# A block of the second layer without the seven-product scheme, and the weights' sums moved into it

## The chip, the cores and the metric

One Trainium2 chip, one core. The metric is the device time of one execution in microseconds (us). The kernel before took 956.48 us, the median of three runs (952.09 to 957.19).

## The reference

A decayed linear attention over 4 batches, 8 heads, 768 positions of 48 channels is followed by two feed-forward layers on 3072 tokens of width 384, with 2048 hidden channels. All inputs and outputs are float32.

```
state = alpha[t, :, None] * state + k[t] (x) v[t];   y[t] = q[t] . state
h = x @ w_in;  g = P3(h) / (1 + |b0||h| + |b1| h^2);  x = g @ w_out      # first layer
h = x @ w_in;  g = h * cos(h);                         out = g @ w_out     # second layer
```

The second layer's weights arrive in a 64-bit format and are converted on the chip.

## The kernel before, in words

**Tiling.** Tokens are cut into six blocks of 512 (`TB`), hidden channels into 16 tiles of 128. One step n of `layers(n)` stands for one hidden tile of one block: steps 0 to 95 are the first layer, steps 96 to 191 the second. Block b of the second layer has the steps 96 + 16b to 111 + 16b, so that block 1 is 112 to 127 and block 2 is 128 to 143. `f` is the place of the step in its block.

**One step.** Each float32 operand is kept as two fp32r words, high and low, and a product of two operands is three passes. `gemm1(n)` writes the hidden tile h(n) into a PSUM bank: nine matmuls of 512 columns in the plain form. `cosine(n)` works on earlier tiles: in the plain form the angle of tile n-1 (ScalarE L78, VectorE L79), and for tile n-2 the sine (ScalarE L744), the product with h (VectorE L746, the last reader of h), the high word (ScalarE L688) and the low word (GpSimd L693). `second(n)` runs `gemm2` for the tile that is `lag` steps back: 4 in the plain form, 5 in the other. A `gemm2` is nine matmuls of 512 columns.

**The seven-product form.** Where `by_seven(n)` holds, two steps (an even one and the odd one after it) share their sub-products: instead of 18 matmuls of 512 columns, `seven` issues six of 512 and 21 of 256. The even step issues six of 256 into bank `r0` ahead of its gemm2 (`seven(n, 0)`), ScalarE moves them out (L604), and after the gemm2 six more go into the same bank (`seven(n, 1)`), which ScalarE moves out as well (L610). The odd step issues the rest into two banks `h_bank(n-1)` and `h_bank(n)`. GpSimd (L605, L616, L618) and VectorE (L627) add what was moved out. The tiles' angle and sine are one step later than in the plain form.

**What the form needs.** Sums of the block's x (`x_sums0` at f = 10, `x_sums1` at f = 14 of the block before; for block 1 on GpSimd at f = 10 of block 0 and at f = 0 of block 1), and sums of the weights, which serve blocks 1 to 5 (`weights_sums(j)` for the pair of tiles 2j, 2j+1). Before, block 0 is plain, block 1 is plain up to f = 3 and in the seven-product form from f = 4, and a whole pair of weights' sums is made in each odd step of block 1: two VectorE additions of 128x256 (L515), four VectorE additions of 128x128 (L519 to L522), then twice a ScalarE copy (L524) and a GpSimd subtraction (L525).

**Weights.** The last weights of the second layer (`w_out`, tiles up to f = 15) are still converted in block 0 and the first steps of block 1: `tick(3)` at the end of each step issues ScalarE L67 and L68, VectorE L72 and L73, the next step ScalarE L187 and GpSimd L196. `words_bank` gives the conversion a free PSUM bank in the steps 100 to 109; later ones work in place in SBUF.

**Order.** The program is issued in the order of the code on every engine, and an engine runs its instructions in that order. A tile that is allocated under a tag whose single buffer an older tile holds can be written first when all readers of the older tile are through, those that come later in the code on other engines too. PSUM banks have one buffer each.

Of the kernel before, what the change touches and what calls it, by code (L numbers as in the profile page):

```python
# [9 lines left out]
F32 = mybir.dt.float32  # L10
F32R = mybir.dt.float32r
# [3 lines left out]
ALU = mybir.AluOpType  # L15
# [3 lines left out]
NC, C = 6, 128  # L19
HP = 4  # L20
NF = DFF // 128
# [18 lines left out]
def attn_then_two_moe(ctx, tc, kqT, aT, vP, w1i, w1o, ma, mb, w2i, w2o, out):  # L40
    nc = tc.nc
# [40 lines left out]
    const = main.enter_context(tc.tile_pool(name="const", bufs=1))  # L82
# [8 lines left out]
    def temp(tag, dtype=F32, shape=(128, TB)):  # L91

        bufs = {"z": 3, "ah": 2, "g": 4, "hi": 3, "lo": 3}[tag]
        return el.tile(list(shape), dtype, tag=tag, name=tag, bufs=bufs)

    def bank(tag, shape=(128, TB), dtype=F32):

        return ps.tile(list(shape), dtype, tag=tag, name=tag)
# [14 lines left out]
    ws = [[wp.tile([128, 2, DM], F32R, name=f"w{s}_{i}") for i in range(NF)] for s in range(2)]  # L113
# [13 lines left out]
    LEAD = NU - 4  # L127
    slot = [0]
# [23 lines left out]
    def words_bank(w):  # L152

        if slot[0] < LEAD:
            return words_t
        if N1 + 3 < slot[0] - LEAD < N1 + NF - 2:
            return bank(f"r{w[2] % 2}", (128, TB), I32)[:, :DM]
        return None

# [297 lines left out]
    N1 = NC * NF  # L457
    N1 = NC * NF
# [5 lines left out]
    def where(n):  # L464
        m, r = divmod(n, N1)
        if n < 2 * H1:
            return 0, *divmod(n, H1)
        if n < 2 * NF:
            blk, f = divmod(n - 2 * H1, NF - H1)
            return 0, blk, H1 + f  # L470
        return m, *divmod(r, NF)
# [8 lines left out]
    HT = TB // 2  # L480
    PASSES = ((0, 0), (0, 1), (1, 0))
    s_in = {}
    x_t = {}
    held = {}

    def by_seven(n):

        m, blk, f = where(n)
        return m == 1 and 0 < blk and (blk > 1 or f >= 4) and (blk < NC - 1 or f < NF - 2)

    def lag(n):

        return 5 if n < N1 or by_seven(n) else 4

    def h_bank(n):
        if n < N1 + NF:
            return bank(f"b{n % 3}")
        return bank((("b1", "b2"), ("r1", "b0"))[n % 2][n // 2 % 2])

    def weights_sums(j):  # L500

        if j == 2:
            held["s1"] = [const.tile([128, 128], F32R, tag=f"s{i}", name=f"s1_{i}") for i in range(2)]
        if j < 6:
            flat = held["kq"][:, 2 * DM * j:2 * DM * (j + 1)].rearrange("p (a b c) -> p a b c", a=2, b=3)
            s = [flat[:, i] for i in range(2)]
        else:
            s = [
                const.tile([128, 3, 128], F32R, tag=f"v{2 * (j - 6) + i}", name=f"s_in{j}{i}") for i in range(2)
            ]  # L510
        first = held["s1"] if j == NF // 2 - 1 else [ws[0][2 * j + 1][:, i, 0:128] for i in range(2)]
        a = temp("z", shape=(128, 4, 128))
        for i in range(2):
            w = ws[0][2 * j + i].bitcast(F32)
            nc.vector.tensor_tensor(  # L515
                out=a[:, 2 * i:2 * i + 2].rearrange("p a b -> p (a b)"), in0=w[:, 0, 0:256], in1=w[:, 1, 0:256], op=ALU.add
            )
        t = temp("g", shape=(128, 4, 128))
        nc.vector.tensor_tensor(out=t[:, 0], in0=a[:, 2], in1=a[:, 3], op=ALU.add)  # L519
        nc.vector.tensor_tensor(out=t[:, 1], in0=t[:, 0], in1=a[:, 0], op=ALU.subtract)  # L520
        nc.vector.tensor_tensor(out=t[:, 2], in0=a[:, 0], in1=a[:, 2], op=ALU.subtract)
        nc.vector.tensor_tensor(out=t[:, 3], in0=a[:, 1], in1=t[:, 1], op=ALU.subtract)  # L522
        for hi, lo, of in ((first[0], first[1], t[:, 0]), (s[0], s[1], t[:, 1:])):
            nc.scalar.activation(out=hi, in_=of, func=AF.Copy)  # L524
            nc.gpsimd.tensor_tensor(out=lo, in0=of, in1=hi.bitcast(F32), op=ALU.subtract)  # L525
        s_in[j] = [[first[i]] + [s[i][:, k] for k in range(3)] for i in range(2)]

    def x_sums0(blk):

        raw = xt[1, blk][:, 1].bitcast(F32)  # L530
        t = [in_p.tile([128, TB], F32, tag="p", name="t") for _ in range(2)]
        eng = nc.gpsimd if blk == 1 else nc.vector
        eng.tensor_tensor(
            out=t[0].rearrange("p (a b) -> p a b", a=2), in0=raw[:, 0:2, HT:],
            in1=raw[:, 0].rearrange("p (a b) -> p a b", a=2), op=ALU.subtract,
        )
        eng.tensor_tensor(out=t[1][:, :HT], in0=raw[:, 1, HT:], in1=t[0][:, :HT], op=ALU.subtract)
        eng.tensor_tensor(out=t[1][:, HT:], in0=raw[:, 1, :HT], in1=t[1][:, :HT], op=ALU.subtract)
        held["t"] = t

    def x_sums1(blk):

        t = held.pop("t")
        if blk == 1:
            held["kq"] = const.tile([128, 5 * 2 * HP * C], F32R, tag="kq", name="s_in")
        tag, words = (("st", 4 * DM), ("a", 3 * HP * (C + 1)))[blk % 2]
        to = const.tile([128, words], F32R, tag=tag, name=f"x_t{blk}")[:, :6 * HT].rearrange(
            "p (a b c) -> p a b c", a=2, b=3
        )
        if 1 < blk < NC - 1:  # L550
            first = [xt[1, blk][:, i, 0, HT:] for i in range(2)]
        else:
            first = [held["kq"][:, 12 * DM + HT * i:12 * DM + HT * (i + 1)] for i in range(2)]
        x_t[blk] = [[first[i]] + [to[:, i, k] for k in range(3)] for i in range(2)]
        for hi, lo, of in (
            (first[0], first[1], t[0][:, :HT]), (to[:, 0, 0], to[:, 1, 0], t[0][:, HT:]),
            (to[:, 0, 1:], to[:, 1, 1:], t[1].rearrange("p (a b) -> p a b", a=2)),
        ):
            nc.scalar.activation(out=hi, in_=of, func=AF.Copy)
            nc.vector.tensor_tensor(out=lo, in0=of, in1=hi.bitcast(F32), op=ALU.subtract)  # L560
# [242 lines left out]
    def all_ok1():  # L803
        cnt = bank("r1", (1, 2 * NU))
        nc.tensor.matmul(cnt, ones, ok.rearrange("p a b -> p (a b)"), start=True, stop=True)
        tot = const.tile([1, 1], F32, name="tot")
        nc.vector.tensor_reduce(tot, cnt, mybir.AxisListType.X, ALU.add)
        nc.vector.tensor_scalar(bad, tot, 128.0 * 2 * NU - 0.5, None, ALU.is_lt)


    def layers(n):
        slot[0] = n + LEAD
        if n == N1 + 4:
            gemm2(N1 - 1)
            done[0] += 1
        if n < 2 * N1:
            gemm1(n)
        if n == NF:
            all_ok0()
        if n == NF + 2:  # L820
            all_ok1()
        m, r = divmod(n, N1)
        blk, f = divmod(r, NF)
        nxt = (m, blk + 1) if blk + 1 < NC else (m + 1, 0)
        at, load = f - 11, f == 8
        if n < NF:
            nxt, at, load = (0, 1), n - 5, n == 3
        elif n < 2 * NF:
            at, load = f - 12, f == 10
        split = 0 <= at < NK and n < 2 * N1 and nxt[0] < 2  # L830
        rational(n)
        cosine(n)
        w_hi()
        if split:
            x_hi(*nxt, at)
        second(n)
        if n < 2 * N1 and by_seven(n) and n % 2 == 0:
            seven(n, 1)
            seven_out1(n)
        if m == 1 and blk == 1 and f % 2:  # L840
            weights_sums((f + 3) // 2 % (NF // 2))
        if m == 1 and nxt[0] == 1 and f == 10:
            x_sums0(nxt[1])
        if n < 2 * N1 and nxt[0] < 2 and load:
            for kk in range(NK):
                x_load(*nxt, kk)
        if split:
            x_lo(*nxt, at)
        if m == 1 and nxt == (1, 2) and f == 0:
            x_sums1(1)  # L850
        if m == 1 and nxt[0] == 1 and nxt[1] > 1 and f == 14:
            x_sums1(nxt[1])
        i = n - (N1 - NF)
        if n < 2 * NF:
            if n > 1:
                w_fetch(2 * NF)
                tick(1 if n > 2 else 0, 1)
        elif n < N1 - NF:
            w_fetch(3 * NF + NO)
            if not split:  # L860
                tick(1, 1)
        elif n < N1:
            w_fetch(4 * NF)
            if i > 3:
                tick(1, 1)
        else:
            w_fetch(4 * NF)
            tick(3 if n > N1 + 3 else 1, 1)
        if 0 <= i < NF:
            w_load(i)  # L870
        if 0 <= i - 6 < NO:
            w_load(NF + i - 6)
        w_lo([nc.gpsimd])
# [248 lines left out]
```

## Time and profile before

| what | value |
|---|---|
| median of three runs | 956.48 us |
| the profiled execution's own time | 956.72 us |
| its span, first to last instruction | 955.0 us |
| VectorE, ScalarE, GpSimd busy | 742.3, 696.4, 730.6 us |
| TensorE waits for ScalarE L604, total of three | 7.8 us |
| TensorE waits for GpSimd L196, one | 3.8 us |
| mean granted clock of TensorE | 0.980 |

The span is what the trace covers; 1.72 us of the execution lie around it. A granted clock of 1.00 is TensorE's upper level, 2.4 GHz, and 0.50 the lower one, 1.2 GHz; a stretch between them has some of both. Matmuls are pipelined, so the start of one is 0.23 us behind the start of the one before although each is drawn 0.40 us long.

### The profile page before, as it was taken

How to read it: one execution, taken by the hardware profiler on the slowest of the kernel's cores; microseconds unless marked ns; L12 is line 12 of the kernel's file. 1: busy time of each engine (PE TensorE's matmuls, PEld its weight loads, DVE VectorE, ACT ScalarE, POOL GpSimd, SP SyncE). 2: the span in 40 equal slices, each digit the busy share in tenths (PEclk: the TensorE clock that was granted, in tenths of full speed). 3: DMA queues.
4: the chain of work that ended last, by engine and by line, in shares of the span. 5: the costliest groups of instructions: out<-in, count | busy, mean ns of one | idle time of the engine just before them, and what ended most of it. 6: DMA issues, size and time to landing. Idle time of an engine off the chain costs nothing. (4 is left out here: it accounts for less than half of the span.)

```text
span 955.0 us, 15338 instructions
## 1 busy us (share of the span) xinstructions
PE 914.6 (96%) x5309; PEld 755.8 (79%) x5309; DVE 742.3 (78%) x1219; ACT 696.4 (73%) x1276; POOL 730.6 (77%) x690
## 2 busy tenths in 40 slices
PE   8797899999999999999999999888899999999997
PEld 7676777878888888888888888677788888888885
DVE  7988979999999989989989656769647658567442
ACT  5888987878779788878888777555566666656663
POOL 5888998989889989879878656576666666666662
PEclk7999999999999999999999999899999999999999
DMA  8999941111113122131265242010010010100001
GB/s 285 312 318 308 295 117 34 34 34 34 66 67 100 34 100 66 67 116 51 63 218 157 78 141 89 18 66 1 1 67 1 1 67 1 66 1 1 34 1 37
DMA packets 47029, 84.68 MB, mean 89 GB/s; under 512 B 5504, under 2 KB 22144, under 8 KB 46944
## 3 DMA queue, kind: packets, MB, share of 16 engines
q1 hardware_dynamic: 46944, 83.62, 27.0%
q8 instruction: 44, 0.72, 0.3%
q14 instruction: 41, 0.34, 0.1%
HBM read 63.15 MB, written 20.45 MB: 88 GB/s over the span
## 5 line engine op out<-in xcount | busy, mean ns | idle before, releaser
L658 PE MATMUL acc<-hi,w 128*128 128x512 f32 x1152 | 393.0, 396 | 3.8 <-POOL w L196 3.8
L693 POOL TENSOR_TENSOR lo<-g,hi 128x512 fp32r<-128x512 f32 x192 | 257.5, 1341 | 102.6 <-ACT hi L688 96.2
L642 PE MATMUL b<-x,w 128*128 128x512 f32 x1053 | 266.5, 398 | 0.6 <-DVE g L711 0.5
L658 PEld LDWEIGHTS acc<-hi,w 128*128 128x128 f32 x1152 | 217.3, 189 | 52.6 <-POOL w L196 4.2
L642 PEld LDWEIGHTS b<-x,w 128*128 128x128 f32 x1053 | 198.2, 189 | 50.0 <-DVE g L711 2.1
L658 PE MATMUL acc<-lo,w 128*128 128x512 f32 x576 | 228.1, 396 | 0.0
L688 ACT ACTIVATE hi<-g 128x512 fp32r<-128x512 f32 x192 | 121.3, 632 | 98.9 <-DVE g L724 51.5
L719 POOL TENSOR_TENSOR z<-z,ah 128x512 f32<-128x512 f32 x96 | 127.2, 1324 | 8.0
L658 PEld LDWEIGHTS acc<-lo,w 128*128 128x128 f32 x576 | 108.6, 188 | 23.1
L746 DVE TENSOR_TENSOR g<-ah,b 128x512 f32<-128x512 f32 x76 | 51.9, 682 | 70.2 <-ACT ah L744 67.8
L79 DVE SCALAR_TENSOR_TENSOR ah<-z,b 128x512 f32<-128x512 int32 x76 | 52.0, 684 | 42.9 <-ACT z L78 42.6
L720 DVE TENSOR_TENSOR g<-g,b 128x512 f32<-128x512 f32 x96 | 65.4, 682 | 25.0 <-ACT g L717 24.3
L718 POOL TENSOR_SCALAR z<-ah,cq 128x512 f32<-128x512 f32 x96 | 74.9, 780 | 1.1 <-ACT ah L716 1.1
L717 ACT ACTIVATE g<-b,cq 128x512 f32<-128x512 f32 x96 | 74.6, 777 | 0.0
L724 DVE SCALAR_TENSOR_TENSOR g<-g,cq,r 128x512 f32<-128x512 f32 x96 | 71.0, 740 | 0.1
L711 DVE SCALAR_TENSOR_TENSOR g<-g,cq,b 128x512 f32<-128x512 f32 x96 | 70.8, 738 | 0.0
L744 ACT ACTIVATE ah<-ah,half_pi 128x512 f32<-128x512 f32 x96 | 68.7, 716 | 0.0
L728 ACT ACTIVATE r<-z,lnb 128x512 f32<-128x512 f32 x96 | 66.7, 695 | 1.8 <-POOL z L719 1.6
L713 DVE SCALAR_TENSOR_TENSOR r<-z,r 128x512 f32<-128x512 f32 x96 | 65.8, 686 | 0.0
L708 DVE SCALAR_TENSOR_TENSOR z<-z,r 128x512 f32<-128x512 f32 x96 | 65.1, 678 | 0.0
L716 ACT ACTIVATE ah<-b 128x512 f32<-128x512 f32 x96 | 56.5, 588 | 7.5 <-PE b L642 7.1
L568 PE MATMUL b<-x,w 128*128 128x256 f32 (+1 forms) x276 | 61.8, 355 | 0.0
(161 smaller groups left out, 1614.3 us busy)
## 6 DMA issues: line engine op xcount, KB each, us to landing
kq<-kqT SPq DMA_DIRECT2D x24, 512.0 KB, 5.5
raw<-w2i SPq DMA_DIRECT2D x16, 384.0 KB, 3.0
w<-wd SPq DMA_DIRECT2D x16, 384.0 KB, 3.1
raw<-w2o SPq DMA_DIRECT2D x16, 384.0 KB, 3.1
v<-vP SPq DMA_DIRECT2D x24, 192.0 KB, 5.4
x<-x0d SPq DMA_DIRECT2D x18, 256.0 KB, 3.5
x1d<-o SPq DMA_DIRECT2D x18, 256.0 KB, 2.1
x<-x1d SPq DMA_DIRECT2D x18, 256.0 KB, 3.7
```

The source lines that it names most:

```text
L642: nc.tensor.matmul(h, ws[0][f][:, w, ks], x[:, xx, kk, :], start=i == 0, stop=i == 8)
L658: nc.tensor.matmul(acc[k], ws[1][f][:, w, ks], d[g], start=first and i == 0, stop=last and i == 2)
L688: nc.scalar.activation(out=t["hi"], in_=t["g"], func=AF.Copy)
L693: eng.tensor_tensor(out=t["lo"], in0=t["g"], in1=t["hi"].bitcast(F32), op=ALU.subtract)
L711: nc.vector.scalar_tensor_tensor(g, g, cq[:, 3:4], two["h"], ALU.add, ALU.mult)
L713: nc.vector.scalar_tensor_tensor(r, z, -2.0 / LN_S, r, ALU.add, ALU.mult)
L717: nc.scalar.activation(out=g, in_=h, func=AF.Identity, scale=cq[:, 5:6], bias=cq[:, 4:5])
L718: nc.gpsimd.tensor_scalar(zz, ah, cq[:, 1:2], cq[:, 0:1], ALU.mult, ALU.add)
L719: nc.gpsimd.tensor_tensor(out=zz, in0=zz, in1=ah, op=ALU.mult)
L724: nc.vector.scalar_tensor_tensor(g, g, cq[:, 2:3], r, ALU.add, ALU.mult)
L728: nc.scalar.activation(out=r, in_=two["z"], func=AF.Ln, scale=LN_S, bias=lnb)
L744: nc.scalar.activation(out=t["r"], in_=t["r"], func=AF.Sin, bias=half_pi)
```

## The change

Block 1 is plain in all its steps (`by_seven` asks for a block above 1, and `h_bank` rotates over three banks up to step 127). The sums of x for block 1 are no longer made. The weights' sums begin at step 115 (f = 3 of block 1) and take two steps a pair: the odd step makes the two large additions on VectorE and the four small ones on GpSimd, the even step after it the copies on ScalarE and the subtractions on GpSimd. The last of the eight pairs ends at step 130. `words_bank` gives a PSUM bank up to step 126.

```diff
-        if N1 + 3 < slot[0] - LEAD < N1 + NF - 2:
+        if N1 + 3 < slot[0] - LEAD < N1 + 2 * NF - 1:
             return bank(f"r{w[2] % 2}", (128, TB), I32)[:, :DM]
...
-        return m == 1 and 0 < blk and (blk > 1 or f >= 4) and (blk < NC - 1 or f < NF - 2)
+        return m == 1 and 1 < blk and (blk < NC - 1 or f < NF - 2)
...
     def h_bank(n):
-        if n < N1 + NF:
+        if n < N1 + 2 * NF:
             return bank(f"b{n % 3}")
         return bank((("b1", "b2"), ("r1", "b0"))[n % 2][n // 2 % 2])
 
-    def weights_sums(j):
-
-        if j == 2:
+    def weights_sums0(j):
+
+        a = temp("z", shape=(128, 4, 128))
+        for i in range(2):
+            w = ws[0][2 * j + i].bitcast(F32)
+            nc.vector.tensor_tensor(
+                out=a[:, 2 * i:2 * i + 2].rearrange("p a b -> p (a b)"), in0=w[:, 0, 0:256], in1=w[:, 1, 0:256], op=ALU.add
+            )
+        held["sums"] = t = temp("g", shape=(128, 4, 128))
+        nc.gpsimd.tensor_tensor(out=t[:, 0], in0=a[:, 2], in1=a[:, 3], op=ALU.add)
+        nc.gpsimd.tensor_tensor(out=t[:, 1], in0=t[:, 0], in1=a[:, 0], op=ALU.subtract)
+        nc.gpsimd.tensor_tensor(out=t[:, 2], in0=a[:, 0], in1=a[:, 2], op=ALU.subtract)
+        nc.gpsimd.tensor_tensor(out=t[:, 3], in0=a[:, 1], in1=t[:, 1], op=ALU.subtract)
+
+    def weights_sums1(j):
+
+        if j == 0:
+            held["kq"] = const.tile([128, 5 * 2 * HP * C], F32R, tag="kq", name="s_in")
             held["s1"] = [const.tile([128, 128], F32R, tag=f"s{i}", name=f"s1_{i}") for i in range(2)]
...
-        t = temp("g", shape=(128, 4, 128))
-        nc.vector.tensor_tensor(out=t[:, 0], in0=a[:, 2], in1=a[:, 3], op=ALU.add)
...
+        t = held.pop("sums")
         for hi, lo, of in ((first[0], first[1], t[:, 0]), (s[0], s[1], t[:, 1:])):
             nc.scalar.activation(out=hi, in_=of, func=AF.Copy)
             nc.gpsimd.tensor_tensor(out=lo, in0=of, in1=hi.bitcast(F32), op=ALU.subtract)
...
-        if m == 1 and blk == 1 and f % 2:
-            weights_sums((f + 3) // 2 % (NF // 2))
-        if m == 1 and nxt[0] == 1 and f == 10:
+        at_sums = n - N1 - NF - 3
+        if 0 <= at_sums < NF:
+            (weights_sums0, weights_sums1)[at_sums % 2](at_sums // 2)
+        if m == 1 and nxt[0] == 1 and nxt[1] > 1 and f == 10:
             x_sums0(nxt[1])
...
-        if m == 1 and nxt == (1, 2) and f == 0:
-            x_sums1(1)
```

## Rows read from the trace of the kernel before

**Rows 1.** The page's part 1: busy time, share of the span, instructions.
```profile
PE 914.6 (96%) x5309; PEld 755.8 (79%) x5309; DVE 742.3 (78%) x1219; ACT 696.4 (73%) x1276; POOL 730.6 (77%) x690
```
**Rows 2.** Waits of TensorE: us in total, times, longest us.
```profile
PE r L568 <- ACT q L604: 7.8, 3, 2.7
PE acc L658 <- POOL w L196: 3.8, 1, 3.8
```
**Rows 3.** Windows: stretch, its us, busy us (x instructions) by engine, TensorE clock.
```profile
core 0: us, PE busy (x) PEld busy (x) DVE busy (x) ACT busy (x) POOL busy (x), PEclk, DMA share, GB/s
...
596.96:601.15 4.19, 4.19 (x19) 3.38 (x18) 3.25 (x5) 2.51 (x7) 1.76 (x2) 1.00 0.26 77
...
605.36:614.99 9.63, 5.88 (x20) 4.36 (x19) 6.74 (x12) 5.95 (x12) 5.71 (x6) 0.77 0.00 0
614.99:620.23 5.24, 5.24 (x19) 4.19 (x18) 4.18 (x9) 1.99 (x5) 3.53 (x4) 0.78 0.00 0
```
**Rows 4.** Windows over pairs of seven-product steps: 120, 124, 128 and 130.
```profile
636.35:646.77 10.42, 7.79 (x38) 6.69 (x36) 8.18 (x18) 5.57 (x11) 6.96 (x8) 0.84 0.00 0
...
654.84:667.14 12.30, 9.88 (x47) 8.24 (x46) 11.53 (x20) 7.14 (x15) 8.80 (x8) 0.86 0.00 0
...
675.20:687.77 12.57, 9.85 (x47) 8.24 (x45) 9.07 (x17) 6.58 (x12) 8.17 (x8) 0.86 0.01 1
687.77:695.83 8.06, 8.06 (x47) 7.00 (x45) 3.72 (x6) 4.63 (x8) 5.33 (x5) 1.00 0.00 0
```
**Rows 5.** GpSimd's timeline: start, us, line, tile, [idle before <- releaser].
```profile
573.97 1.31 POOL L533 TENSOR_TENSOR t<-x 128x512 f32<-128x512 f32 x1
...
600.27 1.29 POOL L693 TENSOR_TENSOR lo<-g,hi 128x512 fp32r<-128x512 f32 x1 [2.43 <-ACT hi L688]
601.53 1.21 POOL L196 TENSOR_TENSOR w<-st,w 128x384 fp32r<-128x384 f32 x1
...
610.47 1.31 POOL L196 TENSOR_TENSOR w<-st,w 128x384 fp32r<-128x384 f32 x1
```
**Rows 6.** VectorE's timeline: a conversion in a bank, one in place, x's sums.
```profile
588.29 0.55 DVE L72 SCALAR_TENSOR_TENSOR r<-st,r 128x384 int32<-128x384 int32 x1
...
592.11 1.44 DVE L72 SCALAR_TENSOR_TENSOR st<-st,raw 128x384 int32<-128x384 int32 x1 [1.49 <-ACT raw L68]
...
601.77 1.85 DVE L560 TENSOR_TENSOR x_t<-t,x_t 128x256 fp32r<-128x256 f32 x2
```
**Rows 7.** ScalarE's timeline at steps 116 and 123.
```profile
621.54 0.59 ACT L604 ACTIVATE q<-r 128x512 f32<-128x512 f32 x1
...
657.82 0.31 ACT L524 ACTIVATE s<-g 128x128 fp32r<-128x128 f32 x1 [2.04 <-DVE g L519]
```
**Rows 8.** All engines' timeline where the odd step 117 begins.
```profile
623.74 1.20 PE L568 MATMUL b<-x,w 128*128 128x512 f32 x6
624.00 0.60 ACT L610 ACTIVATE z<-r 128x512 f32<-128x512 f32 x1 [0.86 <-PE r L568]
624.49 0.71 ACT L744 ACTIVATE ah<-ah,half_pi 128x512 f32<-128x512 f32 x1
...
625.31 0.69 DVE L746 TENSOR_TENSOR g<-ah,b 128x512 f32<-128x512 f32 x1 [1.97 <-ACT ah L744]
```
**Rows 9.** TensorE's timeline in the attention: two of its idle stretches.
```profile
31.44 0.67 PE L336 MATMUL u<-v,g 128*64 128x48 f32 x16 [1.01 <-DVE s L346]
...
43.18 0.67 PE L336 MATMUL u<-v,g 128*64 128x48 f32 x16 [2.95 <-DVE pc L261]
```
**Rows 10.** Windows behind those idle stretches; the clock is before DMA share.
```profile
31.00:34.00 3.00, 2.56 (x48) 2.37 (x48) 2.55 (x10) 2.97 (x8) 3.00 (x4) 1.00 0.72 158
...
44.00:50.00 6.00, 6.00 (x50) 5.11 (x51) 3.92 (x10) 5.08 (x11) 4.32 (x6) 0.50 0.95 305
```
**Rows 11.** The weights' sums by line: duration ns min/median/max.
```profile
L515 DVE TENSOR_TENSOR z<-w x16: 410/581/1518, 605.8 to 677.7; 128x256 f32<-128x256 f32 x16
...
L525 POOL TENSOR_TENSOR s_in<-g,s_in x8: 996/1004/1110, 609.5 to 679.8; 128x384 fp32r<-128x384 f32 x8
L525 POOL TENSOR_TENSOR w<-g,w x7: 453/623/627, 608.3 to 678.9; 128x128 fp32r<-128x128 f32 x7
```

More of the change, by code (lines that the diff above doesn't have):

```diff
@@ L511, in weights_sums @@
         first = held["s1"] if j == NF // 2 - 1 else [ws[0][2 * j + 1][:, i, 0:128] for i in range(2)]
[L512 to L517, printed above, removed]
-        t = temp("g", shape=(128, 4, 128))
-        nc.vector.tensor_tensor(out=t[:, 0], in0=a[:, 2], in1=a[:, 3], op=ALU.add)
-        nc.vector.tensor_tensor(out=t[:, 1], in0=t[:, 0], in1=a[:, 0], op=ALU.subtract)
-        nc.vector.tensor_tensor(out=t[:, 2], in0=a[:, 0], in1=a[:, 2], op=ALU.subtract)
-        nc.vector.tensor_tensor(out=t[:, 3], in0=a[:, 1], in1=t[:, 1], op=ALU.subtract)
+        t = held.pop("sums")
         for hi, lo, of in ((first[0], first[1], t[:, 0]), (s[0], s[1], t[:, 1:])):
@@ L531, in x_sums0 @@
         t = [in_p.tile([128, TB], F32, tag="p", name="t") for _ in range(2)]
-        eng = nc.gpsimd if blk == 1 else nc.vector
-        eng.tensor_tensor(
+        nc.vector.tensor_tensor(
             out=t[0].rearrange("p (a b) -> p a b", a=2), in0=raw[:, 0:2, HT:],
@@ L536, in x_sums0 @@
         )
-        eng.tensor_tensor(out=t[1][:, :HT], in0=raw[:, 1, HT:], in1=t[0][:, :HT], op=ALU.subtract)
-        eng.tensor_tensor(out=t[1][:, HT:], in0=raw[:, 1, :HT], in1=t[1][:, :HT], op=ALU.subtract)
+        nc.vector.tensor_tensor(out=t[1][:, :HT], in0=raw[:, 1, HT:], in1=t[0][:, :HT], op=ALU.subtract)
+        nc.vector.tensor_tensor(out=t[1][:, HT:], in0=raw[:, 1, :HT], in1=t[1][:, :HT], op=ALU.subtract)
         held["t"] = t
@@ L543, in x_sums1 @@
         t = held.pop("t")
-        if blk == 1:
-            held["kq"] = const.tile([128, 5 * 2 * HP * C], F32R, tag="kq", name="s_in")
         tag, words = (("st", 4 * DM), ("a", 3 * HP * (C + 1)))[blk % 2]
@@ L549, in x_sums1 @@
         )
-        if 1 < blk < NC - 1:
+        if blk < NC - 1:
             first = [xt[1, blk][:, i, 0, HT:] for i in range(2)]
```

## The prediction

> **What bounds the kernel now.** I began with the page's engines: TensorE's matmuls cover 96% of the span, the next engine 78% [rows 1]. So the time is TensorE's work plus its stalls. The waits of TensorE, read next, name four stalls in the layers that exceed 2 us: three before line L568 that end with ScalarE's L604, 7.8 us together, and one before L658 that ends with GpSimd's L196, 3.8 us [rows 2]. The timeline put all four around the steps that change, so I laid windows over them.
>
> A plain step takes 4.20 us: step 112 starts at 596.96 and step 114 at 605.36, 8.40 for two. Steps 114 and 115 then take 9.63 and 5.24, 6.47 more than two plain steps [rows 3]. An undisturbed pair of seven-product steps takes 8.06, as at 687.77; the pairs from steps 120, 124 and 128 take 10.42, 12.30 and 12.57 [rows 4]. Each loss is larger than its wait, because the granted clock is 0.84 to 0.86 in these windows and 0.77 and 0.78 in those of steps 114 and 115: the matmuls behind an idle stretch ran partly at 1.2 GHz. The pair of step 128 loses 4.51 us with a wait of 2.7, so the clock took 1.8; at steps 114 and 115 it took about 2.7 (6.47 less 3.8).
>
> Steps 116 to 127 lie between 620.23 [rows 3] and 675.20 [rows 4]: 54.97 us.
>
> **The change part by part.**
>
> *Plain steps for 116 to 127.* Twelve plain steps are 50.40 us instead of 54.97: 4.57 less. Of that, the form itself goes the other way: six pairs at 8.40 instead of 8.06 cost 2.04. What is won is the stalls. The stall of step 120 is made by the change of lag from 4 to 5: in that step no gemm2 is due, so nothing lies between the two halves that share bank r0, and TensorE waits for L604. Those of steps 124 and 128 come from ScalarE: L524 of the odd step before stands ahead of L604 and waits, 2.04 us at 657.82, for VectorE's small additions [rows 7]. A plain step has no L604 and needs a tile's words only four steps later, so a late ScalarE there reaches no matmul at once.
>
> *The stall of step 114.* The low word of the w_out tile for gemm2 at f = 14 is written by GpSimd at 610.47 to 611.78. The one before began at 601.53, so 8.94 us passed where TensorE's step took 4.20 [rows 5]. In between, VectorE made x's sums for block 1 (1.85 for two of the three) and a weights' sum, and GpSimd waited for both chains; two conversions had run in place, 1.44 against 0.55 in a bank [rows 6]. After the change all of that is gone from steps 106 to 114: the three GpSimd instructions (the first 1.31 [rows 5]), three copies and three subtractions of x's sums, the weights' sums of step 113, and the in-place conversions. With an interval of 4.20 the word would be done at 601.53 + 4.20 + 1.31 = 607.0, and TensorE asked for it at 611.8 - 3.8 = 608.0 [rows 2]; the earlier intervals shrink too, so I expect no wait: 6.47 less. Bounds: 6.47 if it goes, 0 if the chain is as late for another reason.
>
> *The weights' sums, later and in two steps.* Their VectorE and ScalarE instructions are the same but for the four small additions, which go to GpSimd. No row shows such an addition there; the nearest, L525 of the same 128x128, takes 0.45 to 0.63 with a median of 0.62, and 128x384 takes 1.00 [rows 11]. I take 0.62. GpSimd's work for two plain steps is then 2 x 1.29 for L693 [rows 5], 0.62 + 1.00 for L525 and 4 x 0.62: 6.68 of 8.40, so it stays beside TensorE, at nothing. If that cover is gone, the adds cost up to what they take (E below); a gain from a lighter VectorE is left out, since no plain step waits for it. VectorE has for two plain steps four instructions of 0.69 (L746 and L79; the row of L746 [rows 8]) and two L515 of 0.41 to 1.52 [rows 11], 5.8 at most of 8.40. Steps 122 to 127 carry x's sums and splits for block 2 besides, as before. No moved piece issues a DMA; the queue of SP is not passed.
>
> *A new wait at step 129.* `h_bank(127)` is now `b1` (127 mod 3 is 1), and `h_bank(128)` is `b1` too. Bank b1 is written at the start of step 129, before the last reader of tile 127's h, which is VectorE's L746 of the same step. TensorE must wait for it, with gemm2(125) behind it in its queue. The chain is read from step 117: TensorE goes on at 623.74, ScalarE starts L610 at 624.00, L744 at 624.49, and L746 runs from 625.31 to 626.00 [rows 8]. There nobody waited for that; here it is 626.00 - 623.74 = 2.26, with 0.08 to be seen. After L610 now stand the two L524 of the pair that ends in step 128, one of them 0.31 [rows 7], the other of 384 columns and so between that and the 0.60 of L610. That is 0.91 at most; since L744 begins 0.11 before L610 ends, I count 0.7 (an estimate). The idle time is 3.04. The clock falls behind it, as behind the stall of 2.95 in the attention, where it was 0.50 for the next 6 us [rows 9, 10]; 1.8 to 2.7 by the cases above, I take 1.9, and 4.9 in all. Bounds: 0, if L746 came sooner than I read, and 5.7.
>
> *The lag moves to step 132.* There no gemm2 is due now. The pair loses 2.10 of work (half of 4.20), which the pair of step 120 lost before, and TensorE waits for L604. The block's outputs stand ahead of it on ScalarE, as at step 116, where L604 ran from 621.54 to 622.13 [rows 7] while the pair had begun at 620.23 [rows 3]. Its first six matmuls are as much as three of the 18 in a step of 4.20, 0.70: with 0.07 for the signal 622.20 - 620.93 = 1.27 idle. An idle stretch of 1.01 left the clock at 1.00 [rows 9, 10], so I add nothing for it; 1.8 is the other bound.
>
> *The sum.* Steps 114 and 115: -6.47. Steps 116 to 127: -4.57. Steps 128 to 131: 12.57 + 8.06 = 20.63 [rows 4] becomes 16.12 + 4.9 = 21.02: +0.39. Steps 132 and 133: 8.06 becomes 8.06 - 2.10 + 1.27 = 7.23: -0.83. Together -11.5. The profiled execution took 956.72 (955.0 and 1.72 around it), 0.24 above the median of 956.48; 956.72 - 11.5 = 945.2.
>
> **The rivals.**
>
> *B, no wait at step 129.* For it: L744 and L746 need nothing of step 129 but their place behind L610. Against: that place is fixed by the code, and L610 ends after TensorE is ready. Time: 945.2 - 4.9 = 940.3.
>
> *C, one or two stalls are left in steps 122 to 128.* VectorE makes x's sums for block 2 there, and L604 of step 128 follows. For it: the stalls of 124 and 128 sat here. Against: ScalarE no longer waits for the small additions in the same step. Each costs what they did, 4.3: 949.5 or 953.8.
>
> *D, the conversion is still late at step 114.* For it: it had under 1 us to spare with an interval of 4.20. Against: what lengthened the intervals is gone. Time: 945.2 + 6.47 = 951.7, half of this on either side of the bound below.
>
> *E, GpSimd's additions hold VectorE: slower.* In the rows L515, with both operands in SBUF, takes 0.41 to 1.52 for one shape [rows 11]. If every addition on GpSimd holds VectorE for its 0.62, eight pairs of four are 19.8 us; if all of it came to TensorE the time would be 965.0. It is slower than before by over 0.5% only if 16.1 of the 19.8 come through. Against: VectorE has 8.40 - 5.8 = 2.6 us to spare in a pair, and 2.5 are asked; only around steps 122 to 127 is there too little.
>
> The Trainium skill (SBUF — State Buffer, section "Who interferes with whom") speaks for E: a VectorE instruction with two SBUF inputs and a GpSimd instruction that reads SBUF exclude each other for a whole instruction, while one with at most one SBUF input is free of this. By the first half the additions on GpSimd would cost E's price at worst; by the second, L746 and L79, which read h from PSUM, go on, and the sum stays at 945.2. The trace bears out that an instruction with two SBUF inputs varies (0.41 to 1.52) and L746 shows 0.69.
>
> **How the numbers follow.** A 0.62, B 0.08, C 0.18 (0.14 one stall, 0.04 two), D 0.07, E 0.05. The likeliest gives 945.2. The range of 939.5 to 951.5 takes in B, A with its bounds and one stall of C, and leaves out two stalls, over half of D, and E, about 0.13. A measurement of this kernel can tell about 0.5% from no change, 4.8 us: faster means under 951.7. A, B, one stall of C and half of D are faster: 0.87; two stalls and the other half of D the same: 0.08; E slower: 0.05.
>
> **What would show it.** In the changed kernel's waits of TensorE, L658 behind L196 is gone, and steps 112 to 128 follow each other by 4.20 with the clock at 1.00. At step 129 a wait of about 3 us for VectorE's L746 stands before L568, with a clock below 1.00 behind it. At step 132 a wait of about 1.3 us for L604. L525 and the additions fit into GpSimd's steps with idle time left. The prediction is wrong if TensorE waits in steps 114 to 128, if step 129 shows no wait, or if the stretch from step 134 on changes its 8.06 a pair.

## The result, and the profile after

The changed kernel took 942.39 us, the median of four runs (940.65 to 943.57), against 955.63 for the four runs of the kernel before that stood beside them (952.09 to 957.19): a ratio of 0.9865 with a 95% interval of 0.9832 to 0.9898. The forecast was 945.2. Four more executions, beside a second set of the kernel before, are under E1.

The profiled execution took 940.65, its span is 938.8, the mean granted clock 0.993. The changed kernel's line numbers have moved: L568 of before is L570, L604 is L606, L610 is L612, L658 is L660, L693 is L695, L744 is L746, L746 is L748; L515 is L505, the four small additions are L509 to L512, L524 and L525 are L529 and L530.

TensorE's waits in the layers answer to [rows 2]; two of over 1 us are left, and both are new:

```profile
PE b L570 <- DVE g L748: 2.8, 1, 2.8
...
PE r L570 <- ACT q L606: 1.1, 1, 1.1
```

The windows answer to [rows 3, 4]. They are steps 112 and 113, 114 and 115, 116 to 127, and the pairs of 128, 130 and 132; the columns are those of before.

```profile
core 0: us, PE busy (x) PEld busy (x) DVE busy (x) ACT busy (x) POOL busy (x), PEclk, DMA share, GB/s
594.20:602.60 8.40, 8.40 (x38) 6.77 (x37) 4.63 (x9) 6.05 (x12) 4.57 (x4) 1.00 0.15 48
602.60:611.00 8.40, 8.40 (x38) 6.77 (x37) 2.86 (x6) 3.49 (x6) 5.27 (x7) 1.00 0.00 0
611.00:661.40 50.40, 50.40 (x218) 40.61 (x216) 31.25 (x47) 29.08 (x56) 35.15 (x46) 1.00 0.10 32
661.40:672.46 11.06, 8.30 (x47) 7.04 (x45) 3.75 (x6) 4.06 (x8) 8.63 (x13) 1.00 0.00 0
672.46:680.52 8.06, 8.06 (x47) 7.00 (x45) 3.08 (x5) 4.51 (x9) 4.87 (x7) 1.00 0.01 2
680.52:687.83 7.31, 6.24 (x38) 5.37 (x37) 5.04 (x9) 5.72 (x10) 6.34 (x7) 1.00 0.62 215
```

From the start of step 112 to the start of step 134 these are 93.63 us. Before it was 106.93 (596.96 to 703.89, the end of an undisturbed pair of 8.06 that starts at 695.83 [rows 4]). So the steps that change give 13.30 in these two executions. The medians differ by 13.24 here but by 10.9 under E1 (953.71 against 942.78), so that the close agreement is chance in part. The profiled execution of before is one of its longer ones: its other executions took 949.76 to 957.87. The two profiled executions differ by 16.07; the other 2.76 lie ahead of step 112 (594.20 against 596.96). They lie even ahead of step 106, since steps 106 to 111 take 25.2 us in both, and so in code that the change leaves as it was; E1 to E11 show the start of step 112 between 592.2 and 598.1.

GpSimd now has the conversion's last low words (L196) at the pace of TensorE's step, 4.18 apart, where before 8.94 passed [rows 5]; the four small additions behind them take 0.46 each:

```profile
600.62 1.02 POOL L196 TENSOR_TENSOR w<-st,w 128x384 fp32r<-128x384 f32 x1
603.56 1.29 POOL L695 TENSOR_TENSOR lo<-g,hi 128x512 fp32r<-128x512 f32 x1 [1.92 <-ACT hi L690]
604.80 1.02 POOL L196 TENSOR_TENSOR w<-st,w 128x384 fp32r<-128x384 f32 x1
...
609.00 0.46 POOL L509 TENSOR_TENSOR g<-z 128x128 f32<-128x128 f32 x1
609.54 0.46 POOL L510 TENSOR_TENSOR g<-g,z 128x128 f32<-128x128 f32 x1
```

The new wait at step 129 is the chain that the prediction read at step 117 [rows 8], with the two copies of the sums (L529) in it. All engines' timeline:

```profile
664.54 0.51 PE L570 MATMUL r<-x_t,s_in 128*128 128x256 f32 x3
665.15 0.60 ACT L612 ACTIVATE z<-r 128x512 f32<-128x512 f32 x1 [1.25 <-PE r L570]
665.64 0.30 ACT L529 ACTIVATE w<-g 128x128 fp32r<-128x128 f32 x1
665.84 0.51 ACT L529 ACTIVATE s_in<-g 128x384 fp32r<-128x384 f32 x1
...
666.25 0.71 ACT L746 ACTIVATE ah<-ah,half_pi 128x512 f32<-128x512 f32 x1
...
667.07 0.69 DVE L748 TENSOR_TENSOR g<-ah,b 128x512 f32<-128x512 f32 x1 [2.97 <-ACT ah L746]
...
667.81 0.73 PE L570 MATMUL b<-x,w 128*128 128x512 f32 x2 [2.76 <-DVE g L748]
```

### The profile page after: what moved, and what is told of

Same layout as the page of the kernel before. It is cut to its first block, busy times and chain, and to the rows that moved or that the text cites. A ratio compares the mean times of both kernels' runs of the same rounds, so it can differ in the third digit from the quotient of the medians.

```text
span 938.8 us, 15168 instructions
## 1 busy us (share of the span) xinstructions
PE 906.9 (97%) x5255; PEld 746.8 (80%) x5255; DVE 713.1 (76%) x1172; ACT 688.8 (73%) x1261; POOL 723.7 (77%) x701
## 4 chain that ended last, share of the span: by engine, by line
PE 80%; DVE 6%; ACT 5%; DMA 4%; issue 2%; POOL 2%; SPq 1%; DVEq 0%; ACTq 0%
PE acc L660 40%; PE b L644 26%; PE r L570 6%; PE b L570 6%; DMA x0d<-g 1%; DVE p L253 1%; DMA x<-x0d 1%; DMA spare<-w1i 1%; DVE st L72 1%; DMA spare<-w1o 1%; DVE g L726 1%; ACT g L719 1%; DMA kq<-kqT 1%; DVE g L713 0%; DVE ah L277 0%
## 5 line engine op out<-in xcount | busy, mean ns | idle before, releaser
L660 PE MATMUL acc<-hi,w 128*128 128x512 f32 x1152 | 392.3, 395 | 0.0
L695 POOL TENSOR_TENSOR lo<-g,hi 128x512 fp32r<-128x512 f32 x192 | 257.3, 1340 | 111.9 <-ACT hi L690 105.4
L644 PE MATMUL b<-x,w 128*128 128x512 f32 x1170 | 294.5, 396 | 0.6 <-DVE g L713 0.5
L644 PEld LDWEIGHTS b<-x,w 128*128 128x128 f32 x1170 | 219.2, 188 | 54.8 <-DVE g L713 2.1
L660 PEld LDWEIGHTS acc<-hi,w 128*128 128x128 f32 x1152 | 216.5, 188 | 49.5
L660 PE MATMUL acc<-lo,w 128*128 128x512 f32 x576 | 227.4, 395 | 0.0
L660 PEld LDWEIGHTS acc<-lo,w 128*128 128x128 f32 x576 | 108.2, 188 | 23.2
L748 DVE TENSOR_TENSOR g<-ah,b 128x512 f32<-128x512 f32 x80 | 54.6, 682 | 77.3 <-ACT ah L746 77.3
L79 DVE SCALAR_TENSOR_TENSOR ah<-z,b 128x512 f32<-128x512 int32 x80 | 54.7, 684 | 44.0 <-ACT z L78 43.5
L746 ACT ACTIVATE ah<-ah,half_pi 128x512 f32<-128x512 f32 x96 | 68.6, 716 | 0.0
L731 ACT ACTIVATE r<-r 128x512 f32<-128x512 f32 x96 | 55.9, 582 | 3.1
```

Of the source, the lines that this page charges most:

```text
L644: nc.tensor.matmul(h, ws[0][f][:, w, ks], x[:, xx, kk, :], start=i == 0, stop=i == 8)
L660: nc.tensor.matmul(acc[k], ws[1][f][:, w, ks], d[g], start=first and i == 0, stop=last and i == 2)
L695: eng.tensor_tensor(out=t["lo"], in0=t["g"], in1=t["hi"].bitcast(F32), op=ALU.subtract)
L746: nc.scalar.activation(out=t["r"], in_=t["r"], func=AF.Sin, bias=half_pi)
```

## The experiments

Times are medians. The ratio compares the mean times of a kernel and of the kernel before, measured beside it, and has its 95% interval behind it. In the traces of E5, E7, E8 and E9 L572 is the changed kernel's L570, L608 its L606, L662 its L660 and L750 its L748.

**E1, the changed kernel again.** No edit.

> The changed kernel once more, beside the three below. Both theories expect 942.4 within 2 us and a wait of 2.8 us for L748 at step 129. Theory 1 (the clock behind that wait is a matter of chance between executions): in some execution the clock falls behind it and the time is 1.7 to 1.9 higher. Theory 2 (the clock never falls there): 11.1 us for the pair of step 128 in every profile.

942.78, ratio 0.9897 (0.9858 to 0.9936). The wait is the same 2.76, but in the profiled execution (944.13) the clock fell behind it: the pair of step 128 took 12.60 instead of 11.06. The same pair in E7 and E8 below, one window from each kernel:

```profile
663.02:675.62 12.60, 9.84 (x47) 8.36 (x45) 3.44 (x6) 4.05 (x8) 9.44 (x14) 0.86 0.00 0
```
```profile
665.32:677.94 12.62, 9.86 (x47) 8.32 (x45) 3.56 (x6) 4.05 (x8) 9.43 (x14) 0.86 0.00 0
```
```profile
660.12:672.76 12.64, 9.88 (x47) 8.30 (x45) 3.69 (x6) 4.05 (x8) 9.44 (x14) 0.86 0.00 0
```

With the changed kernel's first profile and E6 (11.07, clock 1.00), that is three of five executions with a wait of 2.76 in which the clock fell. They are executions of four kernels that are alike from step 128 on; only the first profile and E1 are of one and the same program, and the clock fell in one of these two. The pair took 1.54 to 1.58 more with the fall than without it (1.7 to 1.9 were expected). Beyond 8.06 and the 2.76 of the wait it lost 0.24 without the fall and 1.78 to 1.82 with it. Theory 1 holds.

**E2 and E10, banks b1 and b2 exchanged from step 128 on.**

```diff
-        return bank((("b1", "b2"), ("r1", "b0"))[n % 2][n // 2 % 2])
+        return bank((("b2", "b1"), ("r1", "b0"))[n % 2][n // 2 % 2])
```

> Only b1 and b2 are exchanged in h_bank from step 128 on, so that tile 128 no longer takes the bank of tile 127. Theory 1 (the wait at step 129 is the bank's, as predicted): the wait is gone, the pair of step 128 takes 8.06 instead of 11.06, and the time is 3.0 below the changed kernel's (939.4; more where the clock fell). Rival (TensorE waits there for the late elementwise chain as such): the wait moves to step 131 or to L606 and the time stays within 1 us.

> The swapped banks once more, beside the kernel below: 939 within 1.5; a wait of 1.07 at step 132 alone.

938.94, ratio 0.9860 (0.9829 to 0.9891), and the second time 938.26, ratio 0.9829 (0.9801 to 0.9857). Steps 112 to 127 and the pair of step 128 in E10:

```profile
593.24:660.44 67.20, 67.20 (x289) 54.14 (x288) 38.71 (x60) 38.66 (x74) 44.90 (x57) 1.00 0.09 30
660.44:668.50 8.06, 8.06 (x46) 7.00 (x45) 2.62 (x4) 4.06 (x8) 6.39 (x9) 1.00 0.00 0
```

The wait at step 129 is gone, nothing took its place, and the pair has its 8.06. So the wait was the bank's; it cost 3.0 without a fall of the clock and 4.5 with one. The medians of four executions each gave 3.8 (938.94 beside E1's 942.78; 937.91 to 941.04 against 941.39 to 946.56).

**E3 and E11, the lag of 5 from block 1 on besides.**

```diff
-        return 5 if n < N1 or by_seven(n) else 4
+        return 5 if n < N1 or by_seven(n) or N1 + NF <= n < N1 + 2 * NF else 4
```

> As the one before, and block 1's tiles have the lag of 5, so that the step without a gemm2 is step 116, a plain one. Theory 1 (the idle 1.07 us of step 132 comes from the missing gemm2 between the two halves on r0): the wait for L606 at step 132 is gone, no wait at step 116, and the time is 1.07 below the one before (938.3). Rival (the block's outputs ahead of L606 make the wait): a wait of up to 1 us stays at step 132 or 133.

> Swapped banks and the lag of 5 from block 1 on. Theory 1 (the idle at step 132 is worth its 1.07): 1.0 below the kernel above, within what five rounds tell (0.5 to 1.5). Rival (the idle stretch is given back elsewhere): no difference.

938.62, ratio 0.9843 (0.9811 to 0.9876), then 938.32, ratio 0.9828 (0.9800 to 0.9855). The wait for L606 at step 132 is gone, and at step 116 the matmuls of two hidden tiles run on without a gap. TensorE's timeline in E11:

```profile
611.55 4.61 PE L644 MATMUL b<-x,w 128*128 128x512 f32 x18
616.00 0.39 PE L660 MATMUL acc<-hi,w 128*128 128x512 f32 x1
```

This edit doesn't tell the theory from the rival, since it takes away both. In the changed kernel the block's outputs (L683) stand ahead of L606 in step 132, and L606 begins 1.31 behind the pair's start at 680.52. The lag of 5 moves them to step 133, where no L606 is. The changed kernel, then E11:

```profile
680.72 0.60 ACT L683 ACTIVATE o<-acc 128x512 f32<-128x512 f32 x1 [0.78 <-PE acc L660]
...
681.83 0.59 ACT L606 ACTIVATE q<-r 128x512 f32<-128x512 f32 x1
```
```profile
680.93 1.07 ACT L683 ACTIVATE o<-acc 128x512 f32<-128x512 f32 x2
```

E5's step 120 has no gemm2 either, and no outputs: there L608 begins 0.91 behind the start and TensorE waits 0.69. So of the 1.07 some 0.7 are the missing gemm2's, and some 0.4 the outputs' (an estimate from these two starts).

```profile
638.03 0.62 PE L572 MATMUL r<-s_in,w 128*128 128x256 f32 x3 [0.69 <-ACT q L608]
```

From step 112 to step 134 the trace of E11 has 89.89 us (594.75 to 684.64) against 90.63 in E10 (593.24 to 683.87): 0.74 less, not 1.07, since the even step 128 became 0.36 longer (3.52 between its two halves against 3.16). The medians of five and six runs don't show it, 938.26 and 938.32; the runs spread over 2 and 5 us. What is left of 0.74 us in the time stays open.

**E4, the weights' sums in one step, small additions on VectorE.**

```diff
-        nc.gpsimd.tensor_tensor(out=t[:, 0], in0=a[:, 2], in1=a[:, 3], op=ALU.add)
+        nc.vector.tensor_tensor(out=t[:, 0], in0=a[:, 2], in1=a[:, 3], op=ALU.add)
...
-        if 0 <= at_sums < NF:
-            (weights_sums0, weights_sums1)[at_sums % 2](at_sums // 2)
+        if 0 <= at_sums < NF and at_sums % 2 == 0:
+            weights_sums0(at_sums // 2)
+            weights_sums1(at_sums // 2)
```

> The changed kernel with each weights' sum in one step, the small additions on VectorE, as before the change; block 1 stays plain. Theory 1 (the plain form takes the stalls away, since nothing on TensorE waits for ScalarE within a step): 942.4 within 1 us, no wait in steps 115 to 128. Rival (spreading the sums over two steps takes them away): waits of 2.4 to 2.7 us come back behind some of the steps 115 to 129, 4.3 us each; two of them give 951.

942.32, ratio 0.9899 (0.9861 to 0.9937). Steps 112 to 127, and the pair of step 128:

```profile
593.51:660.70 67.19, 67.19 (x290) 54.14 (x288) 47.94 (x87) 38.90 (x74) 33.94 (x32) 1.00 0.09 30
660.70:671.16 10.46, 8.31 (x47) 7.05 (x45) 4.87 (x11) 5.20 (x10) 7.24 (x8) 1.00 0.00 1
```

No stall came back. In a plain block the sums may hold ScalarE as they did before and TensorE doesn't notice. The wait at step 129 is even shorter, 2.15, since no copy of the sums stands behind L612 there. So in a plain block two of the change's parts, the two steps and GpSimd's additions, are worth nothing that can be measured.

**E5, the two-step sums alone, in the kernel before.** `weights_sums` is replaced by the two functions of the change, and block 1 stays in the seven-product form:

```diff
-        if m == 1 and blk == 1 and f % 2:
-            weights_sums((f + 3) // 2 % (NF // 2))
+        at_sums = n - N1 - NF - 1
+        if 0 <= at_sums < NF:
+            (weights_sums0, weights_sums1)[at_sums % 2]((at_sums // 2 + 2) % (NF // 2))
```

> The kernel before with one part of the change alone: the weights' sums over two steps with the small additions on GpSimd (from step 113 on); block 1 stays in the seven-product form from f = 4. Theory 1 (the stalls of steps 124 and 128 are ScalarE waiting for VectorE's additions in the step before): both are gone, 8.7 us, the stall of step 120 shrinks from 2.6 to about 1.3 without a loss of clock, 3.1, and that of step 114 by part of 3.8: 940 to 945. Rival (only the plain form helps): the waits for L604 stay, and the time is 950 or more.

949.64, ratio 0.9953 (0.9935 to 0.9972): a gain of 3.2 us by the medians (from 952.80) and 4.5 by the means, where I had expected 11.8 (8.7 and 3.1) and part of 3.8. Its waits (L529 is the low word of a sum, L750 the product with h, L564 a sum of x) and the windows of the pairs of steps 124 and 126:

```profile
PE acc L662 <- POOL w L196: 3.0, 1, 3.0
PE r L572 <- POOL s_in L529: 2.3, 3, 1.2
...
PE r L572 <- DVE x_t L564: 1.2, 1, 1.2
...
PE r L572 <- ACT q L608: 0.7, 1, 0.7
```
```profile
651.86:662.05 10.19, 8.60 (x46) 7.11 (x45) 8.77 (x12) 5.95 (x12) 9.67 (x14) 1.00 0.01 2
662.05:671.90 9.85, 8.56 (x46) 7.11 (x45) 7.63 (x12) 6.18 (x14) 9.33 (x13) 1.00 0.00 0
```

The long waits for ScalarE are gone, as theory 1 says; that of step 120 is 0.7. But GpSimd, which has L605, L616 and L618 of before in this form, is busy 9.67 and 9.33 in pairs that take 8.06 when undisturbed, and the sums are late for the tile that uses them. The stall of step 114 stays with 3.0; x's sums and the conversions in place are still there, and the first sum of weights begins in step 113.

**E9, the same with the small additions on VectorE.** In E5's `weights_sums0` the four `nc.gpsimd` become `nc.vector`; the subtractions of `weights_sums1` stay on GpSimd.

> The kernel before with the weights' sums over two steps, but the small additions left on VectorE; block 1 in the seven-product form from f = 4. Theory 1 (with the additions on GpSimd, that engine was the bound of a seven-product pair with sums: 9.13 to 9.67 us of work against 8.06): GpSimd's work falls by 4 x 0.46 to about 7.3, no wait for the sums' low words remains, the pairs of steps 124 to 130 take 8.06 to 8.5, and the time is 3 to 5 below that kernel's 949.6: 945 to 947. Rival (the sums come too late in their two steps whoever adds): waits of 0.6 to 1.2 for the low words stay, 949 to 950.

950.05, ratio 0.9967 (0.9945 to 0.9990). GpSimd's work fell as expected (7.67 and 7.46 in the same pairs) and the time did not:

```profile
PE b L572 <- DVE g L750: 3.6, 2, 2.2
PE r L572 <- DVE g L750: 3.4, 3, 1.8
PE acc L662 <- POOL w L196: 2.7, 2, 2.2
...
PE r L572 <- DVE x_t L564: 1.5, 1, 1.5
...
PE r L572 <- POOL s_in L529: 0.7, 2, 0.5
```
```profile
651.76:662.66 10.90, 8.63 (x46) 7.15 (x45) 9.40 (x15) 5.91 (x12) 7.67 (x8) 1.00 0.01 2
662.66:673.62 10.96, 8.56 (x46) 7.12 (x45) 9.05 (x15) 6.19 (x14) 7.46 (x8) 1.00 0.00 0
```

Now VectorE has 9.40 and 9.05 for a pair, and TensorE waits for its products. Theory 1 failed: with GpSimd relieved the other engine is the bound, and the pairs from step 124 on took 10.9 to 11.1. The rival's time came, but not for its reason, as the waits for the low words fell to 0.46 and 0.25. Not every pair with a weights' sum is too full. That of step 118 takes 8.07 here and 8.08 in E5; those of 9.90 and more are from step 122 on, where block 2's sums of x and splits come on top. And part of VectorE's time is no work: the two L505 take 2.45 in the pair of step 124, beside GpSimd's instructions, where the changed kernel has 0.76 with GpSimd idle. The window of step 118's pair, and L505 in that of step 124:

```profile
625.99:634.06 8.07, 8.07 (x46) 7.00 (x45) 6.85 (x12) 4.71 (x9) 5.70 (x7) 1.00 0.00 0
```
```profile
653.90 2.45 DVE L505 TENSOR_TENSOR z<-w 128x256 f32<-128x256 f32 x2
```

So where the sums of weights and of x meet in the seven-product form, one of the two engines was over 8.06 us in both placements tried. A plain pair has 8.40 and none of L605, L616, L618 and L627.

**E6, the old work put back into the changed kernel.** x's sums for block 1 at their old places, the conversions from step 110 in place, and one sum of weights in one step at step 113; nothing uses them.

```diff
+        if n == N1 + NF + 1:
+            dropped_sums()
...
-        if N1 + 3 < slot[0] - LEAD < N1 + 2 * NF - 1:
+        if N1 + 3 < slot[0] - LEAD < N1 + NF - 2:
...
+        if m == 1 and nxt == (1, 2) and f == 0:
+            x_sums1(1)
```

> The changed kernel with the work put back that stood before step 114: x's sums for block 1 at their old places, conversions from step 110 in place, and one weights' sum in one step at step 113, all of it unused. Theory 1 (this work makes GpSimd's L196 late): the wait of about 3.8 us at step 114 comes back and the time is 942.4 + 6.5 = 949. Rival (something else in the change removed it): no wait, 942.4.

946.35, ratio 0.9939 (0.9923 to 0.9956). The stall is back, with a wait of 3.27: step 114 takes 9.14 and step 115 5.28, together 6.02 more than 8.40 (6.47 before [rows 3]), and GpSimd's L196 is 8.65 behind the one before it, nearly the 8.94 of [rows 5]. The median is only 3.5 above E7's and 3.2 above E8's, measured beside the same executions of the kernel before, and not the 6.5 that I expected. The trace is of the longest of the five executions (950.16), and 2.75 of its 6.02 us are the clock behind the wait; the other four were not traced.

```profile
606.06:615.20 9.14, 5.87 (x19) 4.35 (x18) 6.24 (x12) 5.80 (x12) 5.86 (x6) 0.76 0.00 0
615.20:620.48 5.28, 5.28 (x19) 4.22 (x18) 3.21 (x5) 1.27 (x3) 3.90 (x6) 0.77 0.00 0
```
```profile
602.04 1.22 POOL L196 TENSOR_TENSOR w<-st,w 128x384 fp32r<-128x384 f32 x1
...
610.69 1.31 POOL L196 TENSOR_TENSOR w<-st,w 128x384 fp32r<-128x384 f32 x1
```

**E7, only x's sums put back; E8, x's sums and the conversions in place.** The edits are parts of E6's.

> The changed kernel with only x's sums for block 1 put back, unused. They held the chain up by about 1.1 and 1.6 us before. Theory 1 (the stall needs all three pieces): no wait at step 114, 942.4 within 1. Rival (x's sums alone make the stall): a wait of 1 us or more there.

> The changed kernel with x's sums for block 1 and the conversions in place put back, without the weights' sum at step 113. Theory 1: the chain is late by about 1.1 + 1.6 + 3 x 0.5 = 4.2 against 3 to 3.4 us in hand, so a wait between 0 and 1 us at step 114 or 115 and 942.4 to 944. Rival (the sum at step 113 plays no part): the whole wait of 3.8 us is back, 949.

Both have only two executions. E7: 942.86, ratio 0.9893 (0.9847 to 0.9939), no wait for L196. E8: 943.18, ratio 0.9897 (0.9868 to 0.9925), and one wait that is just to be seen, at step 115:

```profile
607.99 0.73 PE L662 MATMUL acc<-hi,w 128*128 128x512 f32 x2 [0.24 <-POOL w L196]
```

Steps 112 to 127 take 67.20 in E7 and 67.92 in E8 (592.20 to 660.12). So x's sums and the conversions use up the time in hand, and the weights' sum of step 113 on top of them makes the stall: all but 0.7 of its 6.0 us come with it. The weights' sum alone, without the other two, was not tried.

## Why the prediction was right

*Steps 114 and 115* were to fall from 14.87 to 8.40 and did. E6 to E8 show the reason that was given, with one thing to correct: the prediction let all the removed work count alike, but it was the sum in step 113, coming on top of the rest, that turned a late chain into a stall. D, a conversion still late, didn't come.

*Steps 116 to 127* were to take 50.40 and took 50.40, with a clock of 1.00. C, a stall left in these steps, didn't come. E4 shows that the plain form alone does it, as the prediction argued: with each sum in one step and the additions on VectorE no stall comes back either. E5 bears out the reading of the stalls of steps 124 and 128 as an order of waiting on ScalarE, since the long waits for L604 went when the order changed. But E5 and E9 also show that the order was not all: with the sums in the seven-product form, and block 2's sums of x in the same steps, first GpSimd and then VectorE was over the pair's 8.06 us. I had not seen that, and expected 940 to 945 of the order's mending by itself. The stall of step 120 was misread. I put it down to the change of lag, but in the kernel before L524 stands ahead of L604 there as well and waits for VectorE, and with this gone E5 idles 0.69 at step 120 where before had 2.63. So most of that stall had the cause of the other two. The sum didn't suffer, since a plain step has neither. ScalarE's timeline before:

```profile
637.16 0.31 ACT L524 ACTIVATE w<-g 128x128 fp32r<-128x128 f32 x1 [2.49 <-DVE g L519]
```

*The small additions* were counted at 0.62 each and took 0.46 in the median (one took 0.90), beside TensorE. E did not come: L748 kept its 0.67 to 0.69 throughout. Here are VectorE and GpSimd in the timeline of the changed kernel:

```profile
616.39 1.96 DVE L505 TENSOR_TENSOR z<-w 128x256 f32<-128x256 f32 x2
...
616.69 1.39 POOL L695 TENSOR_TENSOR lo<-g,hi 128x512 fp32r<-128x512 f32 x1
...
618.28 0.68 DVE L748 TENSOR_TENSOR g<-ah,b 128x512 f32<-128x512 f32 x1
618.44 0.46 POOL L509 TENSOR_TENSOR g<-z 128x128 f32<-128x128 f32 x1 [0.36 <-DVE z L505]
...
622.99 0.76 DVE L505 TENSOR_TENSOR z<-w 128x256 f32<-128x256 f32 x2
```

Two L505 take 0.76 to 1.96, the latter while GpSimd's L695 runs; L748 takes its 0.68 beside L509. The Trainium skill (SBUF — State Buffer, section "Who interferes with whom") has the exclusion of two-input instructions and the freedom of those with one SBUF input; the rows agree with both halves. No wait of TensorE in steps 112 to 127 followed from it.

*Step 129* was to idle 3.04 and idled 2.76, for the reader of the bank that was named (E2); the copies cost 0.6 where 0.7 were counted. The term that was mis-sized is the clock behind it: 1.9 were counted, and in the profiled execution only 0.24 came beyond the idle time, with a clock of 1.00, so that the four steps from 128 took 19.12 instead of 21.02. Where the clock fell, in E1, E7 and E8, 1.78 to 1.82 came, so the price was right and the certainty wrong. The prediction took the fall as sure from three stalls of 2.4 to 2.7 and one of 2.95, all with it; behind the 2.76 it came in some executions only. Which kind of execution was profiled is luck: E1's would have fitted this term closely.

*Step 132* was to idle 1.27 and idled 1.07, with no fall of the clock; the pair took 7.31 where 7.23 was said.

Sum: -11.5 was forecast for steps 112 to 133, and the traces give -13.30. Nearly all of the 1.8 between them stands at step 129: 1.66 for the clock and 0.28 for the shorter idle time. The other 1.1 of the 2.8 us between 945.2 and 942.39 is where the count began: the forecast started from an execution of 956.72, and the four executions of the kernel before beside the changed one have a median of 955.63.

## What to carry to other kernels

A form that saves matmuls has to be charged with all that it asks of the other engines in the steps where it begins; here it saved 2 us in twelve steps, and its preparation cost some 15 in stalls in the profiled execution (steps 114, 124 and 128), so that starting it one block later was faster. When a rotation of banks is extended, look at the step where it meets the next pattern: one exchange of two names was worth 3.8 us by the medians (E2 beside E1), and with it the time was 938.3 (E10), the fastest version here together with E11. A stall that names one engine can have two engines at their limit behind it: moving work from one to the other (E5, E9) then only changes the name.

## What the runs showed of the hardware

The same idle stretch of TensorE, 2.76 us at step 129, was followed by a clock of 1.00 in two executions (the changed kernel's first profile, E6) and by a fall to a mean of 0.86 over the pair of steps in three (E1, E7, E8). The first profile and E1 are of one and the same program. A single profile does not tell what a stall of that size costs; from 0.24 to 1.82 us beyond itself is what was seen.

Two VectorE additions of 128x256 with both operands in SBUF (L505) took 0.76 us with GpSimd idle and up to 2.47 beside its instructions (E9). VectorE's product with one operand in PSUM (L748) stayed at 0.67 to 0.69 in all of the changed kernel.
